# Attention, soft mixture of experts and SwiGLU in one kernel: another order of token blocks and weight chunks in the SwiGLU, and a later start of converting weight chunk 1

## The chip, the cores and the metric

One core of a Trainium2 chip (trn2) runs the whole program; the other cores are idle. The metric is device time in microseconds (us), and the median of several runs counts. TensorE is written PE, its weight loads PEld, VectorE DVE, ScalarE ACT, GpSimd POOL and SyncE SP.

## The reference

Three layers follow one another. The third, in which the change lies, takes 4608 tokens of width 512:

```python
def _moe2_ref(x, w_gate, w_val, w_out):      # w_gate, w_val: 512 x 1536, w_out: 1536 x 512
    g = x @ w_gate
    silu = g * (1.0 / (1.0 + np.exp(-g)))
    val = x @ w_val
    return (silu * val @ w_out).astype(np.float32)
```

Its x comes from the soft mixture of experts, as `c @ slot_out`: c is a softmax of each token over 32 slots, and slot_out has 32 rows. Ahead of that stands attention over chunks of 64 tokens (8 batches, 8 heads, 576 tokens, head width 64). The weights of the SwiGLU are float64.

## The kernel before

**The stages.** Attention and the slot sums fill about the first 130 us, the experts run to about 175 us, and then the SwiGLU runs to the end. The change touches the SwiGLU alone.

**Work of the SwiGLU.** The tokens are cut into nine blocks of 512, the 1536 hidden columns into six chunks of 256. A chunk is two units f, each of 128 hidden columns. One unit of one block (108 in all) is: two matmuls of 512 columns for the gate and the value (`emit_gv`, L818); silu on ACT (L821) and its product with the value on DVE (L822); a split of the product into a high part (ACT, L830) and a low part (POOL, L831) in `emit_hl`; and in `emit_out`, for each of four groups of 128 tokens, three matmuls into one PSUM accumulator (L862 high by high, L863 high by low weight part, L864 low by high). Gate and value need no product of 512 rows for each token: slot_out is multiplied with a chunk's weights once (`emit_g`, L799, split by L781 and L782 into `g_st`).

**Passes.** A pass is one block over the chunks that `SCHED` names for it. Within a pass the accumulators stay in PSUM, which holds five of them (`ps_o`); a pass uses four. At its end they are moved to an SBUF tile `part` of the block: the block's first pass copies (t = 0 and 2 on ACT, L873; t = 1 and 3 on DVE, L871), a later one adds, all four on DVE (L875). Behind the last unit the sums go out by DMA (L878).

**Conversion of the weights.** Float64 weights come in as pairs of integers and are converted on the chip. A chunk has six items: two halves each of gate, value and out weights. An item goes through four stages: `conv_a` (ACT L185, DVE L186 and L187), `conv_b` (ACT L194, DVE L195), `conv_c` (DVE L200, POOL L213) and `conv_d`, which splits it into `whl` (the high part on ACT, L234; the low part L239, on DVE and POOL by turns). `conv_step` moves every item that is on its way by one stage, and may start another, so an item that starts in step n goes through its last stage in step n + 3.

**What sets the order.** The last loop writes the order of all engines by hand; its index n is called a step below. `seq` lists (block, unit) after `SCHED`. Step n issues the gate and value matmuls of entry n, the split of entry n - 1, one `conv_step`, and then the output matmuls of entry n - 2. Every engine works through its list in that order. An item starts in step n as long as

```python
                conv_step(36 - len(conv_q) < RATE * n + R0)
```

that is, while fewer than 0.38 n + R0 items have been started. `conv_until` would put in more stages where a unit's weights were not ready otherwise. Behind the output matmuls `try_g` issues `emit_g` of the next chunk as soon as its gate and value items are done. `pump` puts weight loads on SP's queue as slots of the pool `wp` come free; the `part` tiles take slots of the same pool.

Of the kernel before, what the change touches and what calls it, by code (L numbers as in the profile page):

```python
# [20 lines left out]
NWX = 4  # L21
NSP = 9
RESV = 6
R0 = 7.4
CV_AT = (14,)
LATE = 3
C_AT = (3, 4, 5, 6, 7, 9, 10, 11, 12)
RATE = 0.38
SCHED = [((0, 1, 2, 3, 4), (0,)), ((5, 6, 7, 8), (0, 1)), ((0, 1, 2, 3, 4), (1, 2)), ((5, 6, 7, 8), (2, 3)),
         ((0, 1, 2, 3, 4), (3, 4)), ((5, 6, 7, 8), (4, 5)), ((0, 1, 2, 3, 4), (5,))]  # L30


@with_exitstack
def tile_attn_softmoe_swiglu(
# [214 lines left out]
    def conv_step(start=True):  # L249
        for k, f in (("d", conv_d), ("c", conv_c), ("b", conv_b)):  # L250
            if stage[k]:
                f()
        if start and conv_ready():
            conv_a()
# [13 lines left out]
    with tc.manual_schedule():  # L268
# [617 lines left out]
        seq = []  # L886
        for blocks, cs in SCHED:
            for b in blocks:
# [31 lines left out]
        for n in range(len(seq) + LAG):  # L920
# [9 lines left out]
            if 1 <= n < len(seq):  # L930
                conv_step(36 - len(conv_q) < RATE * n + R0)
            if n > LAG:
# [57 lines left out]
```

## Time and profile before

| | |
|---|---|
| median of 3 runs | 553.43 us (552.24 to 553.47) |
| the profiled execution | 549.49 us, span 547.7 us |
| granted TensorE clock, mean | 0.995 |
| PE busy | 524.8 us (96%), 4405 matmuls |
| DVE busy | 407.1 us (74%), 679 instructions |
| ACT busy | 260.8 us (48%) |
| POOL busy | 253.0 us (46%) |
| L875, adding accumulators to `part`, DVE | 92 times, 57.1 us |
| chain that ended last | PE 87%, DVE 8%, ACT 2% |

Busy time is that of the whole span. A matmul of 512 columns is listed with some 390 ns, but the next one starts about 227 ns after it, since matmuls overlap; the pace is read from starts. A number in brackets behind a row is idle time of that engine just before the instruction, with what ended it.

### The profile page before, as it was taken

What the parts mean: (1) busy time and instruction counts of PE and PEld (TensorE: products, weight loads), DVE (VectorE), ACT (ScalarE), POOL (GpSimd) and SP (SyncE); (2) the same over time, 40 slices, a digit from 0 to 9 for tenths busy, and PEclk for the clock granted to TensorE, in tenths of its full rate; (3) what the DMA queues carried; (4) which work ended last, traced back from release to release, by engine and by line L of the source; (5) the groups of instructions that cost most, each with busy time, mean ns of one, the idle gap of its engine ahead of it and who ended that gap; (6) DMA issues with size and microseconds to landing.
All of it is one profiled execution on the core that took longest, in us unless ns stands there. A gap on an engine that the chain in (4) does not pass through costs nothing.

```text
span 547.7 us, 11078 instructions
## 1 busy us (share of the span) xinstructions
PE 524.8 (96%) x4405; PEld 412.4 (75%) x4405; DVE 407.1 (74%) x679; ACT 260.8 (48%) x508; POOL 253.0 (46%) x252
## 2 busy tenths in 40 slices
PE   7899999988999889999999999999999999999997
PEld 6777878863345668888888878887887888888885
DVE  5788888755665999898898879988898853343564
ACT  1344433342446766666565555555655433333331
POOL 3334344311001575566666756656665644344342
PEclk9999999999999989999999999999999999999999
DMA  8999999999999502020202220222000000222244
GB/s 324 406 358 398 352 394 378 349 415 409 419 418 416 219 1 77 2 77 2 77 1 77 76 79 1 77 77 77 0 1 0 2 1 1 77 78 77 103 181 178
DMA packets 23763, 91.11 MB, mean 166 GB/s; under 512 B 3104, under 2 KB 3104, under 8 KB 17696
## 3 DMA queue, kind: packets, MB, share of 16 engines
q1 hardware_dynamic: 23712, 90.40, 42.8%
q8 instruction: 35, 0.57, 0.4%
q14 instruction: 16, 0.13, 0.1%
HBM read 80.95 MB, written 9.44 MB: 165 GB/s over the span
## 4 chain that ended last, share of the span: by engine, by line
PE 87%; DVE 8%; ACT 2%; issue 1%; DMA 1%; POOL 0%; SPq 0%; ACTq 0%; DVEq 0%
PE o L862 18%; PE o L863 17%; PE o L864 17%; PE v_ps L818 4%; PE g_ps L818 4%; PE xa_ps L365 4%; PE xt_ps L401 3%; PE s_ps L328 3%; PE so_ps L666 3%; PE pt_ps L351 3%; PE h_ps L621 3%; PE gg_ps L799 2%; PE si_ps L466 2%; PE xb_ps L365 1%; PE lt_ps L419 1%
## 5 line engine op out<-in xcount | busy, mean ns | idle before, releaser
L831 POOL TENSOR_TENSOR lo_sb<-s_sb,hi_sb 128x512 fp32r<-128x512 f32 x106 | 140.7, 1327 | 133.9 <-ACT hi_sb L830 130.7
L862 PE MATMUL o<-whl,hi_sb 128*128 128x512 f32 x428 | 167.8, 392 | 2.7 <-DVE part L871 2.5
L864 PE MATMUL o<-whl,lo_sb 128*128 128x512 f32 x428 | 167.0, 390 | 0.5 <-POOL lo_sb L831 0.5
L863 PE MATMUL o<-whl,hi_sb 128*128 128x512 f32 x428 | 167.0, 390 | 0.0
L821 ACT ACTIVATE s_sb<-g_ps 128x512 f32<-128x512 f32 (+1 forms) x110 | 64.7, 590 | 154.3 <-PE g_ps L818 152.1
L822 DVE TENSOR_TENSOR s_sb<-s_sb,v_ps 128x512 f32<-128x512 f32 (+1 forms) x110 | 74.0, 674 | 78.1 <-ACT s_sb L821 76.7
L862 PEld LDWEIGHTS o<-whl,hi_sb 128*128 128x128 f32 x428 | 80.6, 188 | 22.3 <-DVE part L871 4.8
L864 PEld LDWEIGHTS o<-whl,lo_sb 128*128 128x128 f32 x428 | 80.6, 188 | 17.8 <-POOL lo_sb L831 0.9
L863 PEld LDWEIGHTS o<-whl,hi_sb 128*128 128x128 f32 x428 | 80.6, 188 | 16.3
L830 ACT ACTIVATE hi_sb<-s_sb 128x512 fp32r<-128x512 f32 (+1 forms) x110 | 67.6, 616 | 0.8 <-DVE s_sb L822 0.8
L875 DVE TENSOR_TENSOR part<-part,o 128x512 f32<-128x512 f32 x92 | 57.1, 678 | 2.6 <-PE o L864 2.6
L213 POOL TENSOR_TENSOR mt<-mt,ex 128x512 f32<-128x512 f32 x32 | 39.4, 1233 | 29.5 <-PE g_ps L818 14.4
L318 POOL COPY vbd<-vbd 64x520 f32<-64x520 f32 x36 | 22.3, 619 | 65.5 <-DMA vbd<-in_v_dram 53.3
L200 DVE SCALAR_TENSOR_TENSOR ex<-raw,ex 128x512 uint16<-128x512 uint16 x32 | 47.7, 1491 | 0.1
L818 PE MATMUL v_ps<-c_t,g_st 128*128 128x512 f32 (+1 forms) x110 | 42.8, 392 | 3.1 <-ACT s_sb L821 2.5
L818 PE MATMUL g_ps<-c_t,g_st 128*128 128x512 f32 (+1 forms) x110 | 42.4, 388 | 0.1
L353 ACT ACTIVATE pt<-pt_ps 128x512 f32<-128x512 f32 x36 | 19.5, 596 | 36.6 <-PE pt_ps L351 36.6
L195 DVE SCALAR_TENSOR_TENSOR mt<-mt,raw 128x512 f32<-128x512 f32 x32 | 34.6, 1082 | 0.0
L336 DVE TENSOR_REDUCE m<-s_ps 128x16 f32<-128x1024 f32 x18 | 22.0, 1224 | 15.2 <-PE s_ps L328 15.2
L187 DVE TENSOR_SCALAR mt<-raw 128x512 int32<-128x512 int32 x32 | 32.8, 1026 | 0.0
L365 PE MATMUL xa_ps<-vbd,pt 128*64 128x130 f32 x432 | 27.9, 277 | 0.0
L818 PEld LDWEIGHTS v_ps<-c_t,g_st 128*128 128x128 f32 x110 | 20.6, 189 | 8.7 <-ACT s_sb L821 3.9
(138 smaller groups left out, 669.1 us busy)
## 6 DMA issues: line engine op xcount, KB each, us to landing
qk<-in_qk_dram SPq DMA_DIRECT2D x36, 512.0 KB, 6.2
w1t<-in_moe_w_dram SPq DMA_DIRECT2D x16, 1024.0 KB, 8.5
w2t<-in_moe_w_dram SPq DMA_DIRECT2D x15, 1024.0 KB, 14.0
vbd<-in_v_dram SPq DMA_DIRECT2D x36, 260.0 KB, 7.0
out_dram<-part SPq DMA_DIRECT2D x36, 256.0 KB, 2.1
raw<-in_moe_w_out_dram SPq DMA_DIRECT2D x6, 1024.0 KB, 6.1
raw<-in_moe_w_gate_dram SPq DMA_DIRECT2D x5, 1024.0 KB, 4.8
raw<-in_moe_w_val_dram SPq DMA_DIRECT2D x5, 1024.0 KB, 6.5
```

Source lines behind the costliest of these rows:

```text
L200: nc.vector.scalar_tensor_tensor(out=ex, in0=hh, scalar=0x8000, in1=ex, op0=ALU.bitwise_and, op1=ALU.bitwise_or)
L213: nc.gpsimd.tensor_tensor(out=m, in0=m, in1=p, op=ALU.mult)
L365: nc.tensor.matmul(out=banks[n // 3][64 * cc:64 * cc + 64, (n % 3) * 2 * VW:(n % 3 + 1) * 2 * VW], lhsT=pt_t[i][:, j, 64 * cc:64 * cc + 64 ...
L818: nc.tensor.matmul(out=ps[:, k], lhsT=g_st[:, c, gi, ff:ff + 128], rhs=c_blk(b)[:, k], start=True, stop=True)
L821: nc.scalar.activation(out=s[:, k], in_=gp[:, k], func=ACTF.Silu)
L822: nc.vector.tensor_tensor(out=s[:, k], in0=s[:, k], in1=vp[:, k], op=ALU.mult)
L830: nc.scalar.activation(out=hi[:, k], in_=s[:, k], func=ACTF.Copy)
L831: eng.tensor_tensor(out=lo[:, k], in0=s[:, k], in1=hi[:, k].bitcast(F32), op=ALU.subtract)
L862: nc.tensor.matmul(out=a, lhsT=hi[:, ts], rhs=w_hi, start=first, stop=False)
L863: nc.tensor.matmul(out=a, lhsT=hi[:, ts], rhs=w_lo, start=False, stop=False)
L864: nc.tensor.matmul(out=a, lhsT=lo[:, ts], rhs=w_hi, start=False, stop=last)
L875: nc.vector.tensor_tensor(out=p[:, t], in0=p[:, t], in1=a, op=ALU.add)
```

## The change

Two constants differ. `SCHED` lets all nine blocks pass chunk 0 first; after that five and four blocks take turns with one or two chunks. Before, the first turn took five blocks with chunk 0 and the second four blocks with chunks 0 and 1. `R0`, the head start of the conversion in items, falls from 7.4 to 5.9.

```diff
-R0 = 7.4
+R0 = 5.9
...
-SCHED = [((0, 1, 2, 3, 4), (0,)), ((5, 6, 7, 8), (0, 1)), ((0, 1, 2, 3, 4), (1, 2)), ((5, 6, 7, 8), (2, 3)),
-         ((0, 1, 2, 3, 4), (3, 4)), ((5, 6, 7, 8), (4, 5)), ((0, 1, 2, 3, 4), (5,))]
+SCHED = [((0, 1, 2, 3, 4, 5, 6, 7, 8), (0,)), ((0, 1, 2, 3, 4), (1,)), ((5, 6, 7, 8), (1, 2)),
+         ((0, 1, 2, 3, 4), (2, 3)), ((5, 6, 7, 8), (3, 4)), ((0, 1, 2, 3, 4), (4, 5)), ((5, 6, 7, 8), (5,))]
```

By the two tables there were 32 passes (20 of two or four units by blocks 0 to 4, 12 by blocks 5 to 8), and now there are 36. The first unit of chunks 1 to 5 was entry 12, 28, 48, 64 and 84 of `seq`; now it is entry 18, 30, 46, 66 and 82. The items of chunk 1 started in steps 1, 2, 3, 5, 7 and 10; now they start in steps 1, 3, 6, 9, 11 and 14.

**First place: DVE, steps 2 and 3.** Each L822 opens a step; the two L871 copy accumulators of the first pass. Before:

```order
L822 TENSOR_TENSOR s_sb<-s_sb,v_ps 128x512
L195 SCALAR_TENSOR_TENSOR mt<-mt,raw 128x512
L186 TENSOR_SCALAR ex<-raw 128x512
L187 TENSOR_SCALAR mt<-raw 128x512
L822 TENSOR_TENSOR s_sb<-s_sb,v_ps 128x512
L200 SCALAR_TENSOR_TENSOR ex<-raw,ex 128x512
L195 SCALAR_TENSOR_TENSOR mt<-mt,raw 128x512
L186 TENSOR_SCALAR ex<-raw 128x512
L187 TENSOR_SCALAR mt<-raw 128x512
L871 COPY part<-o_2928 128x512
L871 COPY part<-o_2932 128x512
```

Three of these conversion instructions no longer stand ahead of the copies: the first L186 and L187, and the second L195. With the change the same place reads:

```order
L822 TENSOR_TENSOR s_sb<-s_sb,v_ps 128x512
L195 SCALAR_TENSOR_TENSOR mt<-mt,raw 128x512
L822 TENSOR_TENSOR s_sb<-s_sb,v_ps 128x512
L200 SCALAR_TENSOR_TENSOR ex<-raw,ex 128x512
L186 TENSOR_SCALAR ex<-raw 128x512
L187 TENSOR_SCALAR mt<-raw 128x512
L871 COPY part<-o_2928 128x512
L871 COPY part<-o_2932 128x512
```

**Second place: the last half of chunk 2's out weights.** L239 writes its low part. The first to read it is L863 of the fourth unit of a pass: block 0's second pass before (accumulators o_3822), block 5's second pass now (o_3897). Before, on DVE, from step 29 to step 31, in which that L863 stands:

```order
L822 TENSOR_TENSOR s_sb<-s_sb,v_ps 128x512
L239 TENSOR_TENSOR whl<-mt,whl 128x512
L195 SCALAR_TENSOR_TENSOR mt<-mt,raw 128x512
L822 TENSOR_TENSOR s_sb<-s_sb,v_ps 128x512
L200 SCALAR_TENSOR_TENSOR ex<-raw,ex 128x512
L822 TENSOR_TENSOR s_sb<-s_sb,v_ps 128x512
L186 TENSOR_SCALAR ex<-raw 128x512
L187 TENSOR_SCALAR mt<-raw 128x512
L875 TENSOR_TENSOR part<-part,o_3822 128x512
```

With the change, on DVE, step 33, in which that L863 now stands:

```order
L822 TENSOR_TENSOR s_sb<-s_sb,v_ps 128x512
L239 TENSOR_TENSOR whl<-mt,whl 128x512
L195 SCALAR_TENSOR_TENSOR mt<-mt,raw 128x512
L875 TENSOR_TENSOR part<-part,o_3897 128x512
L875 TENSOR_TENSOR part<-part,o_3901 128x512
```

and on PE the same step 33 with its waits:

```order
L818 MATMUL g_ps<-c_t,g_st 128x512 [waits DVE_49]
L818 MATMUL v_ps<-c_t,g_st 128x512 [waits Activation_49]
L862 MATMUL o_3897<-whl,hi_sb 128x512 [waits Activation_49]
L863 MATMUL o_3897<-whl,hi_sb 128x512 [waits DVE_49]
L864 MATMUL o_3897<-whl,lo_sb 128x512 [waits Pool_49]
```

The conversion has moved from two steps ahead of its first use into the step of that use. Step 49 (chunk 3) has the same rows.

**Third place: DVE at the end of a pass of adds, steps 52 and 53.** Here a pass ends behind L200, L186 and L187:

```order
L822 TENSOR_TENSOR s_sb<-s_sb,v_ps 128x512
L195 SCALAR_TENSOR_TENSOR mt<-mt,raw 128x512
L822 TENSOR_TENSOR s_sb<-s_sb,v_ps 128x512
L200 SCALAR_TENSOR_TENSOR ex<-raw,ex 128x512
L186 TENSOR_SCALAR ex<-raw 128x512
L187 TENSOR_SCALAR mt<-raw 128x512
L875 TENSOR_TENSOR part<-part,o_4511 128x512
L875 TENSOR_TENSOR part<-part,o_4515 128x512
L875 TENSOR_TENSOR part<-part,o_4519 128x512
L875 TENSOR_TENSOR part<-part,o_4523 128x512
```

Steps 61 and 69 read the same. Before, a pass of adds near there (steps 50 and 51) read:

```order
L822 TENSOR_TENSOR s_sb<-s_sb,v_ps 128x512
L239 TENSOR_TENSOR whl<-mt,whl 128x2x256
L195 SCALAR_TENSOR_TENSOR mt<-mt,raw 128x512
L822 TENSOR_TENSOR s_sb<-s_sb,v_ps 128x512
L200 SCALAR_TENSOR_TENSOR ex<-raw,ex 128x512
L875 TENSOR_TENSOR part<-part,o_4434 128x512
L875 TENSOR_TENSOR part<-part,o_4438 128x512
L875 TENSOR_TENSOR part<-part,o_4442 128x512
L875 TENSOR_TENSOR part<-part,o_4446 128x512
```

A start of an item (L186, L187) has come between L200 and the adds.

## Rows read from the trace of the kernel before

**Rows 1.** Timeline of PE, steps 4 to 13: start us, us, instruction, [idle before]

```profile
188.92 0.39 PE L818 MATMUL g_ps<-c_t,g_st 128*128 128x512 f32 x1
...
194.93 0.80 PE L862 MATMUL o<-whl,hi_sb 128*128 128x512 f32 x1 [2.52 <-DVE part L871]
...
210.49 2.07 PE L799 MATMUL gg_ps<-whl,so_hl 128*128 128x256 f32 x16
...
221.97 0.39 PE L818 MATMUL g_ps<-c_t,g_st 128*128 128x512 f32 x1
...
225.14 0.39 PE L818 MATMUL g_ps<-c_t,g_st 128*128 128x512 f32 x1
```

**Rows 2.** Windows: PE, PEld, DVE, ACT, POOL busy, granted clock, DMA

```profile
190.00:200.00 10.00, 7.01 (x23) 5.32 (x24) 8.96 (x11) 6.21 (x13) 7.61 (x6) 0.83 0.01 2
```

**Rows 3.** PE's waits, 240 to 548 us: total us, times, longest

```profile
PE v_ps L818 <- ACT s_sb L821: 2.2, 3, 0.7
```

**Rows 4.** Timeline around step 39, where chunk 3's gate comes in

```profile
314.54 2.47 DVE L875 TENSOR_TENSOR part<-part,o 128x512 f32<-128x512 f32 x4
...
316.47 0.50 PE L818 MATMUL v_ps<-c_t,g_st 128*128 128x512 f32 x1 [0.75 <-ACT s_sb L821]
```

**Rows 5.** Timeline of DVE, steps 2 and 3

```profile
188.18 0.41 DVE L186 TENSOR_SCALAR ex<-raw 128x512 uint16<-128x512 uint16 x1
188.52 0.41 DVE L187 TENSOR_SCALAR mt<-raw 128x512 int32<-128x512 int32 x1
...
190.89 0.68 DVE L195 SCALAR_TENSOR_TENSOR mt<-mt,raw 128x512 f32<-128x512 f32 x1
...
194.20 1.28 DVE L871 COPY part<-o 128x512 f32<-128x512 f32 x2
```

**Rows 6.** Groups of DVE, 195 to 450 us: busy us, mean ns, idle before

```profile
L200 DVE SCALAR_TENSOR_TENSOR ex<-raw,ex 128x512 uint16<-128x512 uint16 x29 | 44.8, 1545 | 0.0
L875 DVE TENSOR_TENSOR part<-part,o 128x512 f32<-128x512 f32 x52 | 32.1, 675 | 0.0
L195 DVE SCALAR_TENSOR_TENSOR mt<-mt,raw 128x512 f32<-128x512 f32 x28 | 31.3, 1117 | 0.0
L187 DVE TENSOR_SCALAR mt<-raw 128x512 int32<-128x512 int32 x27 | 29.7, 1099 | 0.0
L239 DVE TENSOR_TENSOR whl<-mt,whl 128x512 fp32r<-128x512 f32 x15 | 16.3, 1085 | 3.5 <-ACT whl L234 3.5
L186 DVE TENSOR_SCALAR ex<-raw 128x512 uint16<-128x512 uint16 x27 | 13.9, 516 | 0.0
```

**Rows 7.** Timeline of step 13: output matmul, then an item's split

```profile
225.82 0.39 PE L863 MATMUL o<-whl,hi_sb 128*128 128x512 f32 x1
...
226.77 0.63 ACT L234 ACTIVATE whl<-mt 128x512 fp32r<-128x512 f32 x1
...
227.44 1.29 DVE L239 TENSOR_TENSOR whl<-mt,whl 128x512 fp32r<-128x512 f32 x1 [0.49 <-ACT whl L234]
```

**Rows 8.** Timeline of DVE, step 36: the same instruction beside an idle POOL

```profile
303.97 0.68 DVE L200 SCALAR_TENSOR_TENSOR ex<-raw,ex 128x512 uint16<-128x512 uint16 x1
```

**Rows 9.** Timeline of DVE, step 15

```profile
233.21 1.80 DVE L200 SCALAR_TENSOR_TENSOR ex<-raw,ex 128x512 uint16<-128x512 uint16 x1
...
236.58 1.28 DVE L871 COPY part<-o 128x512 f32<-128x512 f32 x2
```

**Rows 10.** Timeline of POOL and PE, steps 15 and 16

```profile
233.17 1.29 POOL L831 TENSOR_TENSOR lo_sb<-s_sb,hi_sb 128x512 fp32r<-128x512 f32 x1 [1.88 <-ACT hi_sb L830]
...
234.66 0.39 PE L818 MATMUL g_ps<-c_t,g_st 128*128 128x512 f32 x1
```

**Rows 11.** Timeline of steps 31 and 32, end of a pass of adds

```profile
287.93 0.39 PE L818 MATMUL g_ps<-c_t,g_st 128*128 128x512 f32 x1
...
288.26 2.47 DVE L875 TENSOR_TENSOR part<-part,o 128x512 f32<-128x512 f32 x4
...
289.06 0.42 PE L862 MATMUL o<-whl,hi_sb 128*128 128x512 f32 x1
```

## The prediction

> **What bounds the kernel now.** I read the page's busy table first (PE 96% of the span), then PE's waits, then the timelines of PE and DVE through the SwiGLU, with the order of the instructions beside them. G is the start of a step's first L818. One step is 225.14 - 221.97 = 3.17 us of PE [rows 1], and from step 9 to the end PE keeps this pace almost without a gap. So the 108 steps cannot shrink: the change can only remove or add PE gaps. Two kinds stand in the trace:
> - Steps 4 to 8 go from 188.92 to 210.49 us, where chunk 1's gate (L799) begins: 21.57 us for five steps worth 15.85, a loss of 5.7 us [rows 1]. Its core is a wait of 2.52 us for a copy out of PSUM by DVE [rows 1], and over the ten us around it the granted clock is 0.83 [rows 2]: part of that stretch ran at the lower level, 1.2 GHz, and (1 - 0.83) x 10 = 1.7 us of clock are missing. Some of it fell into the wait itself, so I count 1.4 us of the 5.7 as the clock's.
> - Three waits of L818 of 0.75 us, together 2.2 us [rows 3, 4].
>
> Together 7.9 us lost. This is the most that the change can win.
>
> **The change part by part.**
>
> *1. Fewer conversion instructions at the start: gain.* Ahead of the first DVE copies stood one L186 and L187 more, which start 0.34 us apart, so 0.67 us, and one L195 more (0.60 us from start to start) [rows 5]. Without them the copies begin 1.3 us sooner than 194.20, and PE's wait falls from 2.52 to 1.2 us, and less if POOL's collisions there shorten too. I take 0.9 us, and leave 0.5 us for the small wait for POOL just before. Later in the first nine passes each pass ends with fewer DVE instructions than before, within the 3.17 us of a step. The clock holds, as it did after the waits of 0.75 us. Loss in place of 5.7: 1.4 us (bounds 0.5 and 2.2).
>
> *2. Four more passes: 16 more L875 at 0.68 us* [rows 6], 10.8 us of DVE. What counts is where they fall. In steps 20 to 29 every other step ends a pass of adds, while conversion of chunk 2 goes on. From the means [rows 6], less 0.08 for the overlap of neighbours: L200 1.5, L195 1.05, L186 with L187 1.5, L239 1.0, four L875 2.4, L822 0.6, two copies 1.2. Steps 19 to 26 then hold 4.8 + 1.65 + 4.5 + 3.1 + 4.05 + 3.6 + 4.05 + 2.1 = 27.9 us of DVE for 25.4 us of PE, 2.5 us too much. PE must wait for it through PSUM, since adds use DVE alone where half the copies were ACT's. Step 27 adds 5.5 us of DVE and then L782 of chunk 2's gate, behind four L875. That is the order that made L818 wait 0.75 us in step 39, where L875 began at 314.54 and L818 could go 1.93 us later [rows 4]; here DVE is some 0.7 us later, so 1.4 us. The gates of chunks 3, 4 and 5 now have no adds ahead of L782, so the three waits of 0.75 us go. Loss here: 3.9 us (bounds 1.5 and 5).
>
> *3. Steps 33 and 49: a conversion lands in the step that reads it.* The last out item of chunks 2 and 3 starts in steps 30 and 46, and its `conv_d` stands in steps 33 and 49, where PE reads it right behind that step's gate and value matmuls. ACT's L234 is issued behind silu (L821) of the same step and L830, DVE's L239 behind L234. Step 13 of the trace shows this chain against a step's start at 225.14: L234 ends at 227.40, L239 at 228.73, G + 3.6 [rows 1, 7]. L863 would want to run at 225.82, G + 0.68 [rows 7]. So PE stands 2.9 us in each of the two steps, 5.8 us (bounds: 2.3 each if L239 takes 0.68 as L200 does beside an idle POOL [rows 8], 3.0 with a later start). Queued behind that L863 on PE are the rest of the unit and the next gate matmuls, on which ACT and DVE then wait, so nothing fills the gap.
>
> *4. Steps 53, 61 and 69: four adds behind L200, L186 and L187.* Step 15 has the same order with copies: L200 takes 1.80 us, and the copies begin only at 236.58, 1.92 us into step 16 [rows 9, 10]. For copies this hardly hurt, since ACT made half of them. A pass of adds has less room: in step 32 the first L875 began at G + 0.33, ended about 0.1 us before the L862 that needs its buffer, and that L862 started on time at G + 1.13 [rows 11]. With L875 at G + 1.92 the L862 starts at 1.92 + 0.67 + 0.1 = G + 2.7, a wait of 1.55 us, three times: 4.7 us (bounds 0 and 5).
>
> Here a rule speaks for the change. The length of L200 is that of a collision: 1.80 us in step 15, where POOL's L831 started 0.04 us ahead of it, 0.68 us while POOL stands [rows 8 to 10]. The Trainium skill, "SBUF — State Buffer", section "Who interferes with whom", says that VectorE and GpSimd share a port pair, that the one that starts first holds it for the whole instruction, and that the other is blocked. By that rule an L200 that starts slightly ahead of L831 would go through at once and hold POOL up instead, and part 4 would cost little (a rival, below); the trace agrees with the block, POOL being first.
>
> *5. The clock.* After the 2.52 us wait it fell, for about 1.4 us [rows 1, 2]. The waits of part 3 are 2.9 us each, but with one matmul inside them. Bounds 0 and 2.8; I take one fall of the two, 1.4 us. The Trainium skill, "TensorE: Matmul & The Clock Gate", section "What's actually happening", says that the monitor's window runs freely, not from the kernel's events: by that the same wait may or may not cost the clock, and neither bound is excluded.
>
> *6. At nothing:* SP's list is the same, and a chunk's load now stands at least six steps ahead of its conversion (five before). POOL has the same work. The last four passes, two steps each, end as before, so the tail behind the last matmul stays.
>
> **Sum.** After: 1.4 + 3.9 + 5.8 + 4.7 + 1.4 = 17.2 us lost; before: 7.9. Difference +9.3 us. Against the profiled execution: 549.5 + 9.3 = 558.8 us. That execution is 3.9 us below the median of the three runs, 553.43; carried to the median: 562.7 us.
>
> **The rivals.**
> - *Faster: DVE and POOL seldom collide.* All hangs on the collisions. If conversion instructions run at their short lengths (L200 0.68, L187 0.41 [rows 5, 8]), step 3 costs 0.9, steps 19 to 29 fit in PE's time and leave 0.75, parts 3 and 4 cost 4.6 and 0, and the clock holds: 6.3 against 7.9, 551.8 us. It decides where the mean of L200 falls below about 1 us; before it was 1.55 [rows 6], and POOL does the same work.
> - *No change: the adds find room.* If the passes of parts 2 and 4 stay hidden and only the gate's wait of 0.75 and the two waits of part 3 are new, the sum is 1.4 + 0.75 + 5.8 = 7.95, or 553.5 us. For it: steps 51, 59 and 67, where adds follow L200, show no wait. Against it: in step 32 the first add had 0.1 us to spare [rows 11].
> - *L200 first.* If in steps 53, 61 and 69 L200 starts ahead of L831, it takes 0.68 instead of 1.80 [rows 8, 9], L875 begins 1.1 us sooner, and each wait is 0.45 instead of 1.55: 562.7 - 3.3 = 559.4 us. In step 15 it was only 0.04 us behind [rows 9, 10]; but the mean of 1.55 says that being late is the rule [rows 6].
> - *The clock falls after every wait over 1.2 us*, some seven of them: six more falls of 1.4, 571.1 us. Against it: the waits of 0.75 us did not do it [rows 3, 4].
> - That the change does not do what it says is excluded by the order of the instructions.
>
> **How the numbers follow.** Forecast 0.58, L200 first 0.12, the clock after every wait 0.08, no change 0.11, faster 0.11. Measurements tell this kernel's time from no change at about 0.3%, 1.7 us. Faster 0.11, same 0.11, slower 0.78. All lower bounds at once (6.6 us lost, 552.1 us) belong to the faster case, so the range begins at that of no change, 553.5 us. Its upper end takes the upper bounds (2.2 + 5 + 6 + 5 + 2.8 = 21.0, so +13.1 us, 566.5) and 1.5 us for the spread of the runs: 568 us. It leaves out the faster case and the clock's.
>
> **What would show it.** Right: no wait of 2.5 us near 192 us; L862 and L863 waiting for ACT L234 and DVE L239 in steps 33 and 49; L862 waiting for L875 in steps 23, 25, 53, 61 and 69; 108 L875. Wrong: L863 on time in step 33, which would take part 3 out; L200 with a mean near 0.7 us; or a new wait for a load.

## The result and the profile after

Measured side by side, the kernel before took 551.92 us (median of 6 runs, 549.83 to 553.47) and the changed one 558.52 us (6 runs, 556.54 to 562.39). The ratio is 1.0124, with a 95% interval of 1.0096 to 1.0152: slower, by 6.6 us in the medians. The two profiled executions took 549.49 and 558.31 us with spans of 547.7 and 556.6 us, 8.9 us apart.

One line of the page after cuts the span into 40 slices and gives the granted clock in tenths (9 is 90% or more):

```profile
PEclk9999999999999999999998999899999999999999
```

The clock's two dips stand in the slices of 292 to 306 and 348 to 362 us. PE's waits from 188 us to the end show where the time went (total us, times, longest):

```profile
PE o L862 <- DVE part L875: 4.3, 4, 1.3
PE o L862 <- ACT whl L234: 3.6, 2, 1.8
PE o L863 <- DVE whl L239: 1.6, 2, 0.8
PE o L862 <- DVE part L871: 0.9, 1, 0.9
PE v_ps L818 <- ACT s_sb L821: 0.7, 1, 0.7
```

The one wait of 2.52 us for L871 [rows 1] is now 0.89, and of the three gate waits [rows 3] one is left. In their place stand two waits for L234 and L239 and four for the adds L875. That does not yet price them: after a wait PE also restarts slowly (step 28, with its wait of 0.75 us, lost 1.07). So I measured each step from one start of L818 to the next, and took off 3.17 us for a step and 1.9 us for a gate that stands in it. What is left is lost (us, worked out from the timelines; a step is a trip of the schedule's loop):

| where | before | after |
|---|---|---|
| step 3, the same in both | 0.6 | 0.6 |
| steps 4 to 8: L871 behind conversion | 5.7 | 1.4 |
| two late copies (L871), 0.3 each: steps 16 and 24 before; 12 and 20 after | 0.55 | 0.55 |
| gate waits: steps 40, 56, 72 before; 28 after | 3.2 | 1.1 |
| late adds (L875), step 26 | 0 | 0.6 |
| steps 33 and 49, and 50, where the clock's second fall ends | 0 | 9.5 |
| late adds, step 42 | 0 | 0.2 |
| late adds, steps 54, 62, 70 | 0 | 4.95 |
| sum | 10.0 | 18.9 |

The difference, 8.9 us, is that of the spans of these two executions: nothing moved ahead of the SwiGLU or behind it.

**Start.** The place of rows 1 in the timeline after (start us, us, instruction, [idle before]), DVE and then PE:

```profile
191.80 1.27 DVE L871 COPY part<-o 128x512 f32<-128x512 f32 x2
...
192.53 0.50 PE L862 MATMUL o<-whl,hi_sb 128*128 128x512 f32 x1 [0.89 <-DVE part L871]
```

DVE's copies begin 2.4 us sooner than at 194.20 [rows 5], 2.2 us sooner counted from the start of step 4 (188.92 before, 188.74 now), and the clock holds: the window from 192 to 204 us (busy us of PE, PEld, DVE, ACT and POOL with instructions, granted clock, DMA share, GB/s), against 0.83 in [rows 2], and the same stretch around each of steps 33 and 49:

```profile
192.00:204.00 12.00, 11.47 (x51) 9.49 (x51) 11.76 (x16) 8.85 (x17) 7.31 (x6) 1.00 0.24 89
288.00:300.00 12.00, 9.40 (x33) 7.03 (x32) 9.83 (x12) 3.48 (x6) 4.19 (x5) 0.86 0.00 0
346.00:358.00 12.00, 9.39 (x34) 7.03 (x32) 9.58 (x12) 3.67 (x7) 4.26 (x4) 0.86 0.00 0
```

**Step 33.** The chain of rows 7 in the step that reads its end, in the timeline of all engines:

```profile
288.41 0.39 PE L818 MATMUL g_ps<-c_t,g_st 128*128 128x512 f32 x1
...
288.90 0.60 ACT L821 ACTIVATE s_sb<-g_ps 128x512 f32<-128x512 f32 x1 [1.49 <-PE g_ps L818]
...
290.14 0.63 ACT L234 ACTIVATE whl<-mt 128x512 fp32r<-128x512 f32 x1
...
290.82 0.50 PE L862 MATMUL o<-whl,hi_sb 128*128 128x512 f32 x1 [1.80 <-ACT whl L234]
290.91 1.16 DVE L239 TENSOR_TENSOR whl<-mt,whl 128x512 fp32r<-128x512 f32 x1
...
292.13 0.50 PE L863 MATMUL o<-whl,hi_sb 128*128 128x512 f32 x1 [0.80 <-DVE whl L239]
...
293.76 0.63 PE L862 MATMUL o<-whl,hi_sb 128*128 128x512 f32 x1
```

Silu (L821), the rounded copy of the entry before (L830), the high part (L234) and the low part (L239) come in this order, and L239 ends 3.66 us behind the step's start. L234 started 0.13 us behind the end of L830, when POOL's L213 of the same item was done (290.11), and L239 came straight behind DVE's L822. The last row shows a matmul of 0.63 us where 0.39 is usual: the clock's lower level, 1.2 GHz, just after the two waits.

**Steps 53 and 54.** DVE's timeline at the end of a pass of adds, then POOL's and PE's rows there:

```profile
365.39 1.80 DVE L200 SCALAR_TENSOR_TENSOR ex<-raw,ex 128x512 uint16<-128x512 uint16 x1
367.11 0.41 DVE L186 TENSOR_SCALAR ex<-raw 128x512 uint16<-128x512 uint16 x1
367.44 1.38 DVE L187 TENSOR_SCALAR mt<-raw 128x512 int32<-128x512 int32 x1
368.75 2.47 DVE L875 TENSOR_TENSOR part<-part,o 128x512 f32<-128x512 f32 x4
...
365.35 1.29 POOL L831 TENSOR_TENSOR lo_sb<-s_sb,hi_sb 128x512 fp32r<-128x512 f32 x1 [1.88 <-ACT hi_sb L830]
367.26 1.28 POOL L213 TENSOR_TENSOR mt<-mt,ex 128x512 f32<-128x512 f32 x1 [0.62 <-PE g_ps L818]
...
369.48 0.50 PE L862 MATMUL o<-whl,hi_sb 128*128 128x512 f32 x1 [1.34 <-DVE part L875]
```

L200 starts 0.04 us behind L831, as it did in rows 9 and 10, and takes 1.80 us. The adds that step 53 issues run while PE is in step 54, whose first L818 ran at 366.84: the first add starts 1.91 us into it, and PE waits 1.34 us for the accumulator.

### The profile page after: what moved, and what is told of

Its sections match the earlier page's. It is cut to its first block, busy times and chain, and to the rows that moved or that the text cites. A ratio compares the mean times of both kernels' runs of the same rounds, so it can differ in the third digit from the quotient of the medians.

```text
span 556.6 us, 11094 instructions
## 1 busy us (share of the span) xinstructions
PE 529.5 (95%) x4405; PEld 415.0 (75%) x4405; DVE 419.3 (75%) x695; ACT 260.7 (47%) x508; POOL 251.6 (45%) x252
## 4 chain that ended last, share of the span: by engine, by line
PE 82%; DVE 12%; issue 2%; ACT 2%; DMA 1%; POOL 0%; SPq 0%; ACTq 0%; DVEq 0%
PE o L862 16%; PE o L863 16%; PE o L864 16%; PE xa_ps L365 4%; PE g_ps L818 4%; PE v_ps L818 4%; PE s_ps L328 3%; PE pt_ps L351 3%; PE xt_ps L401 3%; PE so_ps L666 3%; PE h_ps L621 3%; DVE ex L200 2%; PE gg_ps L799 2%; PE si_ps L466 2%; DVE s_sb L822 1%
## 5 line engine op out<-in xcount | busy, mean ns | idle before, releaser
L831 POOL TENSOR_TENSOR lo_sb<-s_sb,hi_sb 128x512 fp32r<-128x512 f32 x106 | 140.0, 1321 | 143.5 <-ACT hi_sb L830 140.3
L862 PE MATMUL o<-whl,hi_sb 128*128 128x512 f32 x428 | 168.8, 394 | 8.8 <-DVE part L875 4.3
L863 PE MATMUL o<-whl,hi_sb 128*128 128x512 f32 x428 | 168.1, 393 | 1.6 <-DVE whl L239 1.6
L821 ACT ACTIVATE s_sb<-g_ps 128x512 f32<-128x512 f32 (+1 forms) x110 | 64.8, 591 | 163.2 <-PE g_ps L818 163.2
L822 DVE TENSOR_TENSOR s_sb<-s_sb,v_ps 128x512 f32<-128x512 f32 (+1 forms) x110 | 73.8, 673 | 69.5 <-ACT s_sb L821 67.7
L862 PEld LDWEIGHTS o<-whl,hi_sb 128*128 128x128 f32 x428 | 80.9, 189 | 30.3 <-DVE part L875 6.5
L863 PEld LDWEIGHTS o<-whl,hi_sb 128*128 128x128 f32 x428 | 80.9, 189 | 18.6 <-DVE whl L239 2.2
L875 DVE TENSOR_TENSOR part<-part,o 128x512 f32<-128x512 f32 x108 | 67.5, 678 | 6.0 <-PE o L864 6.0
L830 ACT ACTIVATE hi_sb<-s_sb 128x512 fp32r<-128x512 f32 (+1 forms) x110 | 67.7, 617 | 0.8 <-DVE s_sb L822 0.8
L213 POOL TENSOR_TENSOR mt<-mt,ex 128x512 f32<-128x512 f32 x32 | 38.6, 1207 | 30.8 <-PE g_ps L818 13.2
L200 DVE SCALAR_TENSOR_TENSOR ex<-raw,ex 128x512 uint16<-128x512 uint16 x32 | 46.8, 1463 | 0.1
L818 PE MATMUL v_ps<-c_t,g_st 128*128 128x512 f32 (+1 forms) x110 | 42.5, 389 | 1.6 <-ACT s_sb L821 1.0
L818 PE MATMUL g_ps<-c_t,g_st 128*128 128x512 f32 (+1 forms) x110 | 42.4, 389 | 0.1
L195 DVE SCALAR_TENSOR_TENSOR mt<-mt,raw 128x512 f32<-128x512 f32 x32 | 39.1, 1223 | 0.0
L187 DVE TENSOR_SCALAR mt<-raw 128x512 int32<-128x512 int32 x32 | 32.8, 1025 | 0.0
L365 PE MATMUL xa_ps<-vbd,pt 128*64 128x130 f32 x432 | 27.9, 277 | 0.0
L818 PEld LDWEIGHTS v_ps<-c_t,g_st 128*128 128x128 f32 x110 | 20.7, 189 | 6.8 <-ACT s_sb L821 1.8
```

Source lines behind the costliest of these rows:

```text
L195: nc.vector.scalar_tensor_tensor(out=m, in0=m, scalar=-7.0, in1=lw.bitcast(F32), op0=ALU.add, op1=ALU.add)
L200: nc.vector.scalar_tensor_tensor(out=ex, in0=hh, scalar=0x8000, in1=ex, op0=ALU.bitwise_and, op1=ALU.bitwise_or)
L365: nc.tensor.matmul(out=banks[n // 3][64 * cc:64 * cc + 64, (n % 3) * 2 * VW:(n % 3 + 1) * 2 * VW], lhsT=pt_t[i][:, j, 64 * cc:64 * cc + 64 ...
L818: nc.tensor.matmul(out=ps[:, k], lhsT=g_st[:, c, gi, ff:ff + 128], rhs=c_blk(b)[:, k], start=True, stop=True)
L821: nc.scalar.activation(out=s[:, k], in_=gp[:, k], func=ACTF.Silu)
L822: nc.vector.tensor_tensor(out=s[:, k], in0=s[:, k], in1=vp[:, k], op=ALU.mult)
```

## The experiments

The theory by then: the loss is three things that the even spacing of the starts brings (the out items' last stage in the step that reads it, three starts just ahead of adds, and the clock behind the first), and not the new order of the passes or its 16 more adds. The rivals: the adds themselves are too much for DVE, so the order costs time wherever conversion stands; or R0 alone did it. Experiments 1 to 3 and 7 and 8 give the step in which each item starts as a list, by the edit

```
- conv_step(36 - len(conv_q) < RATE * n + R0)
+ conv_step(36 - len(conv_q) < 6 + sum(s <= n for s in STARTS))
```

which moves the lines below it by one (L862 is L863 there). The list that equals the changed kernel's rule is 1, 3, 6, 9, 11, 14, 17, 19, 22, 24, 27, 30, 32, 35, 38, 40, 43, 46, 48, 51, 53, 56, 59, 61, 64, 67, 69, 72, 74, 77. "Lost" is the sum of the last section, 18.9 us for the changed kernel; times are medians, and the kernel before took 551.45 us beside experiments 1 to 4 and 551.6 us beside 5 to 8.

### 1. The out items earlier

```
- starts 27, 30, 43, 46
+ starts 26, 28, 42, 44
```

> The changed kernel, but the out items of chunks 2 and 3 start two steps earlier (in 26, 28, 42 and 44 instead of 27, 30, 43 and 46), so that L239 stands in step 31 and 47, two steps ahead of its reader. Theory 1 (the late conversions: in the trace of the changed kernel steps 33 and 49 lost 3.03 us of waiting each and 1.6 to 1.8 us of clock behind it, 9.5 us together): both waits and both clock falls go, 9.5 us less than the changed kernel, which is about the time of the kernel before, within 2 us. Theory 2 (the 16 more additions as such, 10.8 us of DVE): the additions are all still there, so at most 3 us are gained and the run stays some 5 us above the kernel before. A clock that fell for another reason would leave 3.4 us.

Measured: 550.8 us (549.08 to 553.96), ratio 0.9979 [0.9949, 1.0008]; lost 9.5 us. PE's waits:

```profile
PE o L863 <- DVE part L876: 4.3, 4, 1.3
PE o L863 <- DVE part L872: 0.9, 1, 0.9
PE v_ps L819 <- ACT s_sb L822: 0.7, 1, 0.7
```

Four starts, each moved by one or two steps, take out both waits of steps 33 and 49 and both falls of the clock, 9.4 us of the lost sum. In the medians, by the ratios to the kernel before, it is 8.0 us. That alone brings the changed kernel back to the time of the kernel before, its 16 additions still in it.

### 2. Three starts away from the ends of passes

```
- starts 53, 61, 69
+ starts 54, 62, 70
```

> The changed kernel, but three items start one step later (54, 62 and 70 instead of 53, 61 and 69), so that L186 and L187 no longer stand between L200 and four additions. Same 108 additions, same conversion work. Theory 1 (the additions come too late only where three conversion instructions stand ahead of them): the three waits of 1.34 us (1.65 us of a step each) go, 4.9 us less than the changed kernel, some 2 to 4 us above the kernel before; the waits in steps 33 and 49 stay. Theory 2 (DVE has too much work there): the waits move to the neighbouring passes and the time stays within 1 us of the changed kernel.

Measured: 556.03 us (553.68 to 557.73), ratio 1.0068 [1.0037, 1.0099]; lost 13.6 us. PE's waits:

```profile
PE o L863 <- ACT whl L235: 3.6, 2, 1.8
PE o L864 <- DVE whl L240: 1.6, 2, 0.8
...
PE o L863 <- DVE part L876: 0.8, 2, 0.5
```

The three waits of 1.34 us are gone, and 1.2 us come back in steps 58, 66 and 74. Net that is 3.7 us. The rest of the 5.3 us that the lost sum fell by is the clock, which fell after step 49 alone here. (The span of this profile, 555.6 us, falls short of that gain because its step 2 begins 4.4 us later. The page shows a dip of the clock ahead of the SwiGLU, which the other profile lacks: 0.83 from 130 to 140 us, or 1.7 us; what made the rest is open. The lost sum leaves that stretch out.) The windows of steps 33 and 49:

```profile
292.00:304.00 12.00, 9.39 (x41) 7.18 (x40) 10.74 (x13) 4.64 (x9) 5.68 (x5) 1.00 0.00 0
348.00:362.00 14.00, 11.39 (x42) 8.71 (x41) 11.16 (x14) 4.95 (x9) 6.04 (x6) 0.88 0.00 0
```

The same pair of waits, 1.80 and 0.80 us with one matmul between them, cost the clock once and once not. Step 33 without the fall lost 3.2 us; that is the price of the wait alone.

### 3. Both

> Both edits of the two runs before this one. Theory 1: the losses are separate and add up, 14.4 us less than the changed kernel; that is faster than the kernel before by 5 to 7 us (about 546 us), with the old loss of 5.7 us in steps 4 to 8 and the three gate waits gone and the 16 more additions hidden. Theory 2: no faster than the kernel before.

Measured: 547.35 us (545.27 to 548.41), ratio 0.9923 [0.9886, 0.9959]; lost 5.5 us. PE's waits:

```profile
...
PE o L863 <- DVE part L872: 0.9, 1, 0.9
PE o L863 <- DVE part L876: 0.8, 2, 0.5
```

Of the 0.8, 0.49 us came in step 66, behind the moved starts, and 0.28 in step 26. The two edits add up: 13.4 us of the lost sum went, and of the 18.9 us only the start, one gate wait and small ones stay. By the ratios the edits gained 8.0 and 3.1 us alone and 11.1 us together, each within some 2 us. Seven starts of thirty turn the changed kernel from 1.2% slower than the kernel before into 0.8% faster.

### 4. Three low parts left out, to take the collision away

```
- lo = ht2.tile([128, 512], F32R, tag="lo", name="lo_sb")
+ lo = hi if (b, f) in NO_LO else ht2.tile([128, 512], F32R, tag="lo", name="lo_sb")
...
+ if (b, f) in NO_LO:
+     continue
...
+ NO_LO = [gvs[i] for i in (52, 60, 68)]
```

> The changed kernel without POOL's L831 for entries 52, 60 and 68: the low part of three units is left out (the high part is read in its place, so PE has the same matmuls). DVE's instructions and their order are the same. If the additions are late because L200 collides with L831 (the account of the prediction), L200 takes about 0.7 us instead of 1.8 in steps 53, 61 and 69, the additions begin about 1.1 us sooner and each wait of 1.34 us falls to 0.2 to 0.4. If the number of instructions ahead of the additions is the cause and not the collision, L200 stays at 1.8 us and the waits stay at 1.34.

Measured: 557.16 us in one run; steps 54, 62 and 70 lost 0.54 us each where they had lost 1.65. The same place in the timelines of DVE and PE:

```profile
367.53 0.69 DVE L200 SCALAR_TENSOR_TENSOR ex<-raw,ex 128x512 uint16<-128x512 uint16 x1
...
368.47 1.39 DVE L187 TENSOR_SCALAR mt<-raw 128x512 int32<-128x512 int32 x1
369.78 2.47 DVE L877 TENSOR_TENSOR part<-part,o 128x512 f32<-128x512 f32 x4
...
370.51 0.50 PE L864 MATMUL o<-whl,hi_sb 128*128 128x512 f32 x1 [0.23 <-DVE part L877]
```

Without L831, L200 takes 0.69 us instead of 1.80, and PE's wait falls from 1.34 to 0.23 us: 1.11 us each. So the wait needs the collision. By experiment 2 it needs the order as well: there L200 (L201 in that kernel) still took 1.79 us at 368.11, and with L186 and L187 out of the way PE did not wait. L187 itself collides, with POOL's L213: 1.38 us in step 53 and 1.39 here, both times started 0.2 us behind an L213, against 0.41 in [rows 5]. No run takes that collision away. In this run too the clock held after the waits of step 33 (lost 3.2 us) and fell after those of step 49 (4.7 us).

### 5. The new order of passes alone (R0 = 7.4)

```
- R0 = 5.9
+ R0 = 7.4
```

> The new order of passes with the old head start (R0 = 7.4). Starts fall on steps 1, 2, 3, 5, 7 as before, and no item is late; four passes of additions (steps 49, 57, 65, 73) and perhaps step 23 end behind L200, L186 and L187. Theory 1: the old loss of 5.7 us in steps 4 to 8 is back, the waits in steps 33 and 49 are gone, four waits of 1.34 us stand behind steps 49, 57, 65 and 73, no gate waits: some 14 us lost in all against 9.4 in the kernel before and 18.3 in the changed one, so 3 to 6 us above the kernel before. Theory 2 (the 16 additions as such): as slow as the changed kernel.

Measured: 557.95 us (557.62 to 559.51), ratio 1.0101 [1.0048, 1.0154]; lost 15.6 us. PE's waits:

```profile
PE o L862 <- DVE part L875: 8.1, 7, 1.3
PE o L862 <- DVE part L871: 2.2, 1, 2.2
...
```

With everything 1.5 items earlier the waits of steps 33 and 49 do not exist, but seven passes of adds come late for PE, where the changed kernel has four and four or five were expected, and the start keeps its wait, 2.2 us. After it the clock fell again: the window from 194 to 200 us ran at 0.78.

### 6. R0 = 5.9 alone, in the old order

```
- SCHED = [((0, 1, 2, 3, 4, 5, 6, 7, 8), (0,)), ((0, 1, 2, 3, 4), (1,)), ((5, 6, 7, 8), (1, 2)),
-          ((0, 1, 2, 3, 4), (2, 3)), ((5, 6, 7, 8), (3, 4)), ((0, 1, 2, 3, 4), (4, 5)), ((5, 6, 7, 8), (5,))]
+ SCHED = [((0, 1, 2, 3, 4), (0,)), ((5, 6, 7, 8), (0, 1)), ((0, 1, 2, 3, 4), (1, 2)), ((5, 6, 7, 8), (2, 3)),
+          ((0, 1, 2, 3, 4), (3, 4)), ((5, 6, 7, 8), (4, 5)), ((0, 1, 2, 3, 4), (5,))]
```

> The old order of passes with the new head start (R0 = 5.9): the items start in the same steps as in the changed kernel, but chunk 1 is wanted at entry 12 and not 18. Theory 1: the loss in steps 4 to 8 falls from 5.7 to about 1.5 us, but several items are now forced: waits of 3 to 6 us with clock falls about steps 12 to 15 and 30 and 31, and the three gate waits stay: some 25 us lost, 10 to 20 us above the kernel before. So the two constants belong together. Rival (the smaller head start is a gain wherever it stands, the new order is the loss): 4 us below the kernel before.

Measured: 575.71 us (574.8 to 577.53), ratio 1.0421 [1.0365, 1.0476]; lost 33.6 us. The largest of PE's waits:

```profile
PE o L862 <- ACT whl L234: 12.4, 3, 5.4
PE v_ps L818 <- ACT s_sb L821: 2.8, 4, 1.0
...
```

The start loses 1.4 us, as in the changed kernel: that gain is R0's alone. But chunk 1 is wanted from entry 12 of the old order, six entries sooner than in the new one, and out items that are late are converted in the step that reads them, with waits up to 5.4 us. The expectation, some 25 us lost and 10 to 20 us above the kernel before, was too small: 33.6 us were lost and the run was 24 us above. Waits of 3 to 6 us were expected and none was longer; but the clock, which had no price there, was low for long: 0.77 from 224 to 246 us and 0.66 from 299 to 314, worth some 10 us at most.

### 7. The old order, with starts set one by one

The list is 1, 2, 5, 7, 10, 11, 14, 15, 18, 21, 23, 26, 27, 30, 32, 35, 39, 42, 44, 47, 49, 53, 56, 57, 60, 63, 65, 69, 72, 76, with the old SCHED.

> The old order of passes (no additions more) with start steps chosen one by one: never L200 with L186 and L187 ahead of additions, few conversion instructions ahead of the first copies, gates of chunks 3 to 5 in steps without additions, and every item two steps ahead of its reader. Theory 1: of the 9.4 us lost by the kernel before some 2 us remain: 5 to 8 us faster, about 545 us. Rival (the loss at the start is set by the copies themselves and not by the conversion ahead of them): at most 3 us faster.

Measured: 547.17 us (545.63 to 551.03), ratio 0.9925 [0.9892, 0.9958]; lost 5.3 us. PE's waits:

```profile
PE o L865 <- POOL lo_sb L832: 1.3, 3, 0.6
PE o L864 <- POOL whl L240: 0.9, 1, 0.9
```

No wait for an accumulator is listed, and the gates no longer wait. Some 2 us lost and a gain of 5 to 8 us were expected; 5.3 us are lost and 4.4 us were gained; what is listed are waits for POOL, four where the kernel before has one. The time alone does not exclude the rival of at most 3 us (the interval is 2.3 to 6.0 us); the trace does, as the loss of steps 4 to 8 fell from 5.7 to 2.6 us.

### 8. The new order, with starts set one by one

The list is 1, 2, 6, 7, 10, 12, 14, 16, 19, 23, 26, 29, 32, 35, 38, 41, 42, 45, 48, 51, 54, 56, 59, 62, 64, 67, 70, 72, 75, 78, with the new SCHED.

> The new order of passes with start steps chosen by the same rules. Theory 1: the late conversions, the late additions and the gate wait go, some 2 us lost in all: 5 to 8 us faster than the kernel before and within 1.5 us of the run with the old order, since PE's work is the same and the 16 more additions fit beside it. Theory 2 (additions as such): 5 us or more slower than the run with the old order.

Measured: 546.5 us (545.61 to 547.4), ratio 0.9888 [0.9837, 0.9939]; lost 4.4 us. It beats both kernels, by 5.1 us the kernel before beside it. PE's waits:

```profile
PE o L865 <- POOL lo_sb L832: 0.5, 1, 0.5
PE o L863 <- DVE part L876: 0.5, 1, 0.5
```

The other two in the list are of 0.3 us. Some 2 us lost were expected here too.

Experiments 7 and 8 can't be told apart in time (0.7 us, with runs that overlap; their intervals leave some 3 us open in either direction). So no worth of the order of the passes is measurable once the starts are placed in these two ways, and the one wait for an add that experiment 8 lists is 0.5 us: the first rival fell. The second fell with experiment 6: R0 alone costs 24 us in the old order, while in the new one (experiment 5 against the changed kernel) it takes the start's wait out and brings those of steps 33 and 49 in. The two belong together. Neither alone nor both were a gain over the kernel before: 1.010 for the order alone, 1.042 for R0 alone, 1.012 for both.

## Why the prediction was right

The side and the size were right: +9.3 us forecast, +8.9 between the profiled executions, +6.6 in the medians. The last two differ because the profiled execution of the kernel before lies 2.4 us under its median of 551.92, and that of the changed kernel only 0.2 us under its own. As a time, 562.7 us was forecast and 558.5 came; the rival *L200 first*, with 559.4, is nearer. The time does not tell the two apart; the lengths of L200 do (below). And that the sum came out is luck in part: its terms were off in opposite directions (us lost):

| part | forecast (bounds) | measured |
|---|---|---|
| 1 start | 1.4 (0.5 to 2.2) | 1.4 |
| 2 four more passes | 3.9 (1.5 to 5) | 1.7 |
| 3 steps 33 and 49, waits | 5.8 (4.6 to 6) | 6.4, at 3.2 each (experiment 2) |
| 4 steps 53, 61, 69 | 4.7 (0 to 5) | 4.95 |
| 5 clock | 1.4 (0 to 2.8) | 3.1, what is left of 9.5 |
| not counted | 0 | 1.3 (step 3, two late copies, step 42) |
| after | 17.2 | 18.9 |
| before | 7.9 | 10.0 |

1. **Start: right.** The wait fell to 0.89 us where 0.9 was forecast, and the clock held. Of the 2.2 us by which the copies come sooner, 1.3 are the three instructions, as counted; the rest is an L186 that took 1.38 us before and takes 0.42 now, the shorter collision that was named without a price. The 0.5 us set aside for a wait for POOL came only in part (0.2); the restart after the wait filled the place (0.3). Experiments 5 and 6 show that it is R0's work: 2.2 us of wait with the old value, 0.9 with the new one.

2. **Four more passes: the mis-sized term.** The step that failed is the sum by means: "L200 1.5 ... 27.9 us of DVE for 25.4 us of PE". From the L822 of step 19 (241.15) to the end of step 26's L200 (267.09) DVE worked without a pause for 25.9 us. The means hold for the stretch as a whole (L200 1.51 after), but not here: two of the four L200 took 0.68 us, and so did step 22's L239; L186 and L187 took 0.41 each there. Rows of DVE and POOL in steps 24 and 25:

```profile
256.48 2.47 DVE L875 TENSOR_TENSOR part<-part,o 128x512 f32<-128x512 f32 x4
257.89 1.30 POOL L831 TENSOR_TENSOR lo_sb<-s_sb,hi_sb 128x512 fp32r<-128x512 f32 x1 [1.88 <-ACT hi_sb L830]
258.87 0.67 DVE L822 TENSOR_TENSOR s_sb<-s_sb,v_ps 128x512 f32<-128x512 f32 x1
259.46 0.68 DVE L200 SCALAR_TENSOR_TENSOR ex<-raw,ex 128x512 uint16<-128x512 uint16 x1
```

   The adds push L822 and L200 back, L200 comes when POOL's L831 is over (259.19), and takes 0.68 us instead of 1.5. Of the two passes named as signs there, that of step 23 brought no wait and that of step 25 one of 0.30 us, in step 26, which lost 0.6; 2.5 was forecast for these steps in all.

   The gate's wait came in step 28 as forecast, but at 0.75 us instead of 1.4; with its restart the step lost 1.07. Here the mechanism was wrong too:

```profile
271.94 0.60 ACT L821 ACTIVATE s_sb<-g_ps 128x512 f32<-128x512 f32 x1
...
272.59 0.50 PE L818 MATMUL v_ps<-c_t,g_st 128*128 128x512 f32 x1 [0.75 <-ACT s_sb L821]
...
273.23 0.76 DVE L782 TENSOR_TENSOR g_st<-gg_ps,g_st 32x256 fp32r<-32x256 f32 x2
```

   L818 went when ACT's L821 of the same step had ended, at 272.54, and the L782 behind the adds, which the prediction took for the cause, ran only after it. So the wait lasts until silu is done, not until DVE is: it was 0.75 us in all four places of the two kernels. The gates with adds ahead of L782 have it and the others have not; how the adds bring it about stays open.

3. **Steps 33 and 49: right**, and the largest term. L239 ended at 3.66 us behind the step's start (forecast 3.6). The waits themselves hold PE's next matmul back by 3.0 us; the rest of 3.2 is PE's slow restart, which I had left out. Experiment 1 took them out by moving four starts.

4. **Adds behind L200, L186 and L187: right**, by its mechanism too. The wait was 1.34 us where 1.55 was forecast; with the restart each step lost 1.65. Experiment 4 shows that 1.11 us of it hangs on the collision with L831, and experiment 2 that the collision alone, without L186 and L187 ahead of the adds, costs nothing.

5. **Clock: one fall forecast, two came.** One of two was a choice in the middle of the bounds, not a finding; how many come, the runs leave open (four in six equal places). The two waits of 1.80 and 0.80 us took it down in both places of the changed kernel, and in one of two in experiments 2 and 4. Wait and clock together are 9.2 us in the two steps of the profiled execution, of the 18.9 lost.

6. **Before: 7.9 counted, 10.0 there.** Each gate wait of 0.75 us costs 1.06 us of its step with the restart, and 1.1 us in step 3 and in two steps with a late copy stand in both kernels.

The rivals: *L200 first* did not happen. Of 29 runs of L200 from 195 to 465 us, 24 overlapped an L831, which had started first, by 0.04 to 0.38 us, in all of them; the five without overlap took 0.68 us. So its mean stayed at 1.51 us, and *few collisions* fell with it:

```profile
L200 DVE SCALAR_TENSOR_TENSOR ex<-raw,ex 128x512 uint16<-128x512 uint16 x29 | 43.8, 1511 | 0.0
```

*The adds find room* fell in steps 53, 61 and 69, though it was half right in steps 19 to 26. *The clock after every wait over 1.2 us* fell: the three waits of 1.34 us left it alone (window at the end).

## What to carry to other kernels

When a rule of constant rate spreads optional work over a fixed order, look in the order of the instructions for two things before anything else: a result that is made in the very step that reads it, and optional work that stands ahead of the instructions that free an accumulator. Both can be cured by moving a few starts by one or two steps, and seven such moves were worth 2% here, more than the change itself in either direction. Where two engines collide, don't add up mean durations: an engine that falls behind may leave the collision and become faster. And before a wait is scaled with the work in front of it, look which instruction's end it followed.

## What the hardware showed

- **When L831 ends sets when L200 ends.** Two pairs in the changed kernel's timelines of POOL and DVE, at 365 and 373 us (the first L200 stands above, in step 53):

```profile
373.32 1.29 POOL L831 TENSOR_TENSOR lo_sb<-s_sb,hi_sb 128x512 fp32r<-128x512 f32 x1 [3.36 <-ACT hi_sb L830]
...
373.54 1.63 DVE L200 SCALAR_TENSOR_TENSOR ex<-raw,ex 128x512 uint16<-128x512 uint16 x1
```

  L200 ends at 375.17 here, 0.56 us behind the L831 that ends at 374.61; the one of step 53 ends at 367.19, 0.55 us behind 366.64. Over the 24 overlapping pairs it is 0.55 us, with L200 between 1.45 and 1.80 us long and L831 always 1.28 or 1.29. The Trainium skill, "SBUF — State Buffer", section "Who interferes with whom", says that the engine which starts first holds the shared ports for its whole instruction and the other is fully blocked. These rows agree, with POOL first. With DVE first it is POOL that comes later: from 195 to 465 us six L831 started right behind an L186 and took 1.56 us each instead of 1.29. One of them:

```profile
376.53 0.42 DVE L186 TENSOR_SCALAR ex<-raw 128x512 uint16<-128x512 uint16 x1
376.55 1.56 POOL L831 TENSOR_TENSOR lo_sb<-s_sb,hi_sb 128x512 fp32r<-128x512 f32 x1
```

- **The same wait may or may not cost the clock.** In four places with the pair of 1.80 and 0.80 us in experiments 2 and 4 it fell twice, in the changed kernel twice of two. The Trainium skill, "TensorE: Matmul & The Clock Gate", section "What's actually happening", says that the window of the chip's monitor runs freely and is not reset when a kernel starts; four falls in six equal places fit that, but do not show it. A fall cost some 1.5 us (3.1 us for two). The waits of 0.89 and 1.34 us in the changed kernel left the granted clock at 1.00, as the first of the three windows under **Start** and this one around step 53 show:

```profile
364.00:372.00 8.00, 6.66 (x30) 5.20 (x29) 7.23 (x11) 4.04 (x7) 3.96 (x3) 1.00 0.38 131
```
